# Attention feeding a squared-ReLU MLP: first q loads on a second hardware DMA queue, scalar loads moved to GpSimd's queue, last tile stored as 384 and 128 columns

## Chip, cores, metric

One core of one Trainium2 chip. The metric is the device time of one execution in microseconds (us), median over several executions.

## The reference, cut to what matters

```python
# q, k, v: (4, 8, 768, 64) float32; n_global 8, n_local 96
scores = q @ k.T / 8 + bias(head slope, distance)     # ALiBi-like
scores = where(local or global, scores, -1e9)
attn   = softmax(scores) @ v                          # -> x: (3072, 512)
h      = maximum(x @ w_in, 0)                         # w_in (512, 2048)
out    = (s * h*h + b) @ w_out                        # w_out (2048, 512); s, b: one number each
```

## The kernel before

The work is cut into 12 tiles of 256 tokens. Tile 0 is loaded as float32 on SyncE's queue (hardware_dynamic in the trace) and cast on chip. Everything else (v, later q and k, both weights) goes through GpSimd's queue (software_dynamic), where each issue keeps GpSimd busy for 0.6 to 1.0 us in the trace, and is cast from float32 to bfloat16 on the way. The head of the program, in the order of issue:

```python
nc.scalar.preload_act_table_set("natural_log_exp_and_others")
...
for nm, half in (("k", 0), ("q", 0), ("k", 1), ("q", 1)):
    nc.sync.dma_start(raw32[...], first(nm, half))       # 256 KB each, float32
... # masks on GpSimd, then its loads:
load_v(0); load_quads(1, "k"); load_quads(1, "q")
load_w_in(0, 8); load_w_in(1, 8); load_v(1)
for i in range(2, 8): load_w_in(i, 8)                    # 8 pieces of 256 columns
load_quads(2, "k"); load_quads(2, "q"); load_v(2)
for i in range(3): load_w_out(i)
def load_scalars():                                      # one number to 128 partitions
    nc.sync.dma_start(s_bc[:], moe_s.to_broadcast((P, 1)))
    nc.sync.dma_start(b_bc[:], moe_b.to_broadcast((P, 1)))
for h in range(H):
    nc.scalar.activation(diag[:, h, :], ident[:], ACT.Copy, scale=...)
... # cut
idle(9, "av")                     # 9 filler matmuls
cast("k", 0, "act"); T_mm(0, 0, "k"); T_ev(0, 0, "k")    # transpose on TensorE
cast("q", 0, "act"); ...
more_loads()                      # k(3), w_out(3), q(3), v(3), tile 4, GpSimd's queue
load_scalars()
```

`load_scalars` stands late in the program text, but SyncE has nothing to do before it except the four loads, so it issues the scalars right behind them.

In the steady part, `period(j)` computes the scores of tile j, first and second linear layer of earlier tiles, and loads tile j+2. `pace(j)` makes GpSimd wait for an early result of the period. `KO` collects the keys of the previous block on VectorE:

```python
def period(j, items, at, late=None):
    SS(j, (0, 1))                            # scores, exp, times template
    if j + 2 < NJ:
        pace(j)                              # GpSimd copies one element of pts[j, 0]
        load_granule(j + 2)                  # k, k, q, q, v, v on GpSimd's queue
    ...
    A(j, 1); SS(j, (2, 3))
    if j + 1 < NJ: KO(j + 1)                 # ko <- kT, 128x1024 bfloat16, SBUF to SBUF
    ...
def P2_end(j, tb):                           # the very last 128 tokens, in two column parts
    for pool, tag, lo, hi in ((ps_a, "scA", 0, 320), (ps_b, "scB", 320, DM)):
        P2_cols(j, tb, ps[:, 0, :], lo, hi)  # 16 matmuls, one VectorE op, one store
```

The softmax here doesn't subtract the row's maximum and nothing guards it: scores larger than these inputs give would overflow.

Of the kernel before, what the change touches and what calls it, by code (L numbers as in the profile page):

```python
# [10 lines left out]
ACT = mybir.ActivationFunctionType  # L11
# [7 lines left out]
def kernel(  # L19
# [13 lines left out]
    nc = tc.nc  # L33
    P = nc.NUM_PARTITIONS

    B, H, S, D = q.shape
    NG = int(n_global)
    NL = int(n_local)
    DM = H * D
# [14 lines left out]
    QSCALE = 1.0 / float(D) ** 0.5  # L54
# [8 lines left out]
    ps_a = ctx.enter_context(tc.tile_pool(name="ps_a", bufs=1, space=bass.MemoryType.PSUM))  # L63
    ps_b = ctx.enter_context(tc.tile_pool(name="ps_b", bufs=1, space=bass.MemoryType.PSUM))
# [17 lines left out]
    def bg(j):  # L82
        return divmod(j, NGR)
# [13 lines left out]
    def load_rows(j, nm):  # L97
        b, g = bg(j)
        src = q if nm == "q" else k
        t = ldp.tile([P, GB, H, D], BF16, name=f"{nm}nat", tag=f"{nm}nat")  # L100
        nat[nm, j] = t
        for i in range(GB):
            sb = g * GB + i
            nc.gpsimd.dma_start(  # L104
                t[:, i, :, :], src[b, :, sb * P : (sb + 1) * P, :].rearrange("h p d -> p h d")
            )

    def load_v(j):
        b, g = bg(j)
        for i in range(GB):  # L110
            sb = g * GB + i
            nc.gpsimd.dma_start(  # L112
                vaug[b][:, sb, :, 0:D],
                v[b, :, sb * P : (sb + 1) * P, :].rearrange("h p d -> p h d"),
            )

    def load_granule(j):
        load_rows(j, "k")
        load_rows(j, "q")
        load_v(j)  # L120
# [13 lines left out]
    def load_w_out(i, n=4):  # L134
        w = FC // n
        nc.gpsimd.dma_start(
            w_out_bf[:, i * w : (i + 1) * w, :], w_out_view[:, i * w : (i + 1) * w, :]
        )


    nc.scalar.preload_act_table_set("natural_log_exp_and_others")
    raw32 = gpool.tile([P, 2, H, GB * D], F32, name="raw32", tag="gT")
    for nm in "kq":
        nat[nm, 0] = ldp.tile([P, H, GB * D], BF16, name=f"{nm}nat", tag=f"{nm}nat")
# [1 line left out]
    def first(nm, half):  # L146
        src = (q if nm == "q" else k)[0, 4 * half : 4 * half + 4, 0:GT, :]
        return src.rearrange("h (p i) d -> p h (i d)", i=GB)

    for nm, half in (("k", 0), ("q", 0), ("k", 1), ("q", 1)):  # L150
        nc.sync.dma_start(raw32[:, "kq".index(nm), 4 * half : 4 * half + 4, :], first(nm, half))

    def cast(nm, half, eng=None):
        hs = slice(4 * half, 4 * half + 4)
# [6 lines left out]
    ident = const.tile([P, P], BF16, name="ident")  # L161
# [42 lines left out]
    def more_loads():  # L204
        load_rows(3, "k")
        load_w_out(3)
        load_rows(3, "q")
        load_v(3)
        load_granule(4)

    s_bc = const.tile([P, 1], F32, name="s_bc")
    b_bc = const.tile([P, 1], F32, name="b_bc")

    def load_scalars():
        nc.sync.dma_start(s_bc[:], moe_s.to_broadcast((P, 1)))
        nc.sync.dma_start(b_bc[:], moe_b.to_broadcast((P, 1)))


    diag = const.tile([P, H, P], BF16, name="diag")
    for h in range(H):  # L220
        nc.scalar.activation(
            diag[:, h, :], ident[:], ACT.Copy, scale=float(2.0 ** (-8.0 * (h + 1) / H) / QSCALE)
        )

    for b in range(B):
        nc.vector.memset(vaug[b][:, :, :, D : D + 1], 1.0)
# [62 lines left out]
    def T_ev(j, half, nm, eng=None, es=(0, 1)):  # L289
        b, g = bg(j)  # L290
        a = 0 if nm == "k" else 1
        if j not in qT:
            qT[j] = qtp.tile([P, HP, GT], BF16, name="qT", tag="qT")
        e0, e1 = es[0], es[-1] + 1
        n = GB if j == 0 else 4
        src = tps[j, half, nm][:, a, e0:e1, :].rearrange("p e (i t) -> p e t i", i=n)
        hs = slice(2 * half + e0, 2 * half + e1)
        dst = kT[b][:, hs, g * GT : (g + 1) * GT] if nm == "k" else qT[j][:, hs, :]
        dst = dst.rearrange("p e (t i) -> p e t i", i=n)
        if eng is None:  # L300
            nc.vector.tensor_copy(dst, src)
        else:
            nc.scalar.copy(dst, src)
# [64 lines left out]
    def SB_mm(j, hp, which=None):  # L368
        ps = sc_tile(j, hp, which)
        n = ncols(j)  # L370
        c0 = 0 if n == 3 * P else P
        m = base[:].rearrange("p a c -> p (a c)")[:, c0 : c0 + n]
        for hi in range(2):
            nc.tensor.matmul(
                ps[:, hi, 0:n], lhsT=diag[:, 2 * hp + hi, :], rhs=m, start=True, stop=False
            )
# [221 lines left out]
    def P2_cols(j, tb, ps, lo, hi):  # L598
        b, g = bg(j)
        flush()  # L600
        for fc in range(FC):
            nc.tensor.matmul(  # L602
                ps[:, 0 : hi - lo],
                lhsT=gT[j][:, fc, tb * P : (tb + 1) * P],
                rhs=w_out_bf[:, fc, lo:hi],
                start=(fc == 0),
                stop=(fc == FC - 1),
            )
        o_sb = work.tile([P, hi - lo], F32, name="o_sb", tag="o_sb", bufs=5)
        nc.vector.scalar_tensor_tensor(  # L610
            out=o_sb[:],
            in0=ps[:, 0 : hi - lo],
            scalar=s_bc[:],
            in1=bvec[:, lo:hi],
            op0=ALU.mult,
            op1=ALU.add,
        )
        t0 = b * S + g * GT + tb * P
        nc.sync.dma_start(out[t0 : t0 + P, lo:hi], o_sb[:])

    def P2_end(j, tb):
        for pool, tag, lo, hi in ((ps_a, "scA", 0, 320), (ps_b, "scB", 320, DM)):
            ps = pool.tile([P, 2, DM], F32, name="ps_2e", tag=tag)
            P2_cols(j, tb, ps[:, 0, :], lo, hi)

# [24 lines left out]
    T_mm(0, 1, "q", "av", True)  # L650
    T_ev(0, 1, "q", None, (0,))
    T_ev(0, 1, "q", None, (1,))
    more_loads()
    load_scalars()
    SB_mm(0, 3)
    S_mm(0, 2, True)
    S_post(0, 2, True)
# [167 lines left out]
    for j in range(4, NJ):  # L825
# [11 lines left out]
        [(P2, l, 4, 0), (P2, l, 5), (P1, m, 0), (P2, l, 6), (P1, m, 1), (P2, l, 7), (P1, m, 2), (P1, m, 3), (P1, m, 4)]  # L837
        + [(P2, m, 0), (P1, m, 5), (P1, m, 6), (P1, m, 7), (P2, m, 1), (P2, m, 2), (P2, m, 3)]
        + [(P2_end, m, 1)],
        100,  # L840
    )
# [35 lines left out]
```

## Time and profile before

| | before |
|---|---|
| median of 3 runs | 217.13 us (216.68 to 217.26) |
| span in the profile | 215.4 us |
| TensorE busy | 206.1 us, 96% |
| k0, q0, k1, q1 landed (first and second halves of tile 0) | 3.77, 4.65, 6.80, 7.82 us |
| first v piece, first and sixth w_in piece landed | 9.07, 14.19, 23.64 us |

Landing is the issue time plus "issue to landing" of the trace. All times count from the start of the span. In the views PE is TensorE, PEld its weight loads, DVE VectorE, ACT ScalarE, POOL GpSimd, SP SyncE; a q behind an engine is its sequencer, which issues and waits. L12 is line 12 of the kernel.

The page of the kernel before: the span, busy time by engine, the chain's shares by engine, and two DMA issue groups (size of one, median us from issue to landing).

```profile
span 215.4 us, 5089 instructions
PE 206.1 (96%) x2061; PEld 140.6 (65%) x2093; DVE 135.8 (63%) x322; ACT 115.5 (54%) x176; POOL 69.8 (32%) x96
PE 80%; DMA 9%; ACT 3%; POOL 3%; issue 2%; DVE 1%; SPq 1%; POOLq 0%; ACTq 0%
...
raw<-in_k_dram SPq DMA_DIRECT2D x2, 256.0 KB, 4.0
raw<-in_q_dram SPq DMA_DIRECT2D x2, 256.0 KB, 4.4
```

TensorE bounds the kernel. Only the head, where it waits for data, and the tail after its last matmul can shrink by such a change.

The timeline of SyncE's queue in the first 10 us of the kernel before: start us, us, what.

```profile
0.74 0.46 SPq L151 DMA_DIRECT2D raw<-in_k_dram  x1
1.26 0.49 SPq L151 DMA_DIRECT2D raw<-in_q_dram  x1
1.80 0.50 SPq L151 DMA_DIRECT2D raw<-in_k_dram  x1
2.35 0.51 SPq L151 DMA_DIRECT2D raw<-in_q_dram  x1
2.89 0.57 SPq L215 DMA_DIRECT2D s_bc<-in_moe_s_dram  x1
3.50 0.59 SPq L216 DMA_DIRECT2D b_bc<-in_moe_b_dram  x1
```

One issue takes about 0.5 us of the sequencer; the scalars follow the four loads at once.

The chain of waits of the kernel before in its first 40 us: start us, us, what.

```profile
2.49 6.58 DMA vaug<-in_v_dram
9.07 0.28 issue
...
11.36 2.20 POOL w_in_bf L130 x3
13.56 10.08 DMA w_in_bf<-in_moe_w_in_dram
...
23.68 2.81 PE ps L508 x24
```

The chain runs over GpSimd's stream until 23.64 us, not over q and k. The waits of the weight loads (PEld) between 12 and 30 us in the kernel before, total us, times, longest:

```profile
PEld L508 <- DMA w_in_bf<-in_moe_w_in_dram: 0.7, 3, 0.3
```

The DMA queues of the kernel before from 7 to 8 us: packets, MB, share of 16 engines' time. q0 is GpSimd's queue, q1 SyncE's.

```profile
q0 software_dynamic: 425, 0.05, 83.3%
q1 hardware_dynamic: 194, 0.01, 22.6%
```

In this microsecond the scalars' four-byte packets run on q1 beside GpSimd's stream, which moves 425 packets.

The end of VectorE's timeline of the kernel before: the last two instructions, each followed by a store.

```profile
210.77 0.55 DVE L610 SCALAR_TENSOR_TENSOR o_sb<-ps_2e,s_bc,bvec 128x320 f32<-128x320 f32 x1 [1.42 <-PE ps_2e L602]
212.09 0.42 DVE L610 SCALAR_TENSOR_TENSOR o_sb<-ps_2e,s_bc,bvec 128x192 f32<-128x192 f32 x1 [0.77 <-PE ps_2e L602]
```

### The profile page before, as it was taken

The numbers are of one execution on the slowest core, as the hardware profiler recorded it, in microseconds if no ns is written. First come the engines' busy times: TensorE is split into PE (matmuls) and PEld (weight loads), VectorE is DVE, ScalarE is ACT, GpSimd is POOL, SyncE is SP. The second block draws the span as 40 slices with busy tenths as digits, with TensorE's granted clock in tenths as the row PEclk, the third lists the DMA queues.
The fourth block names the chain that finished last, engine by engine and source line by source line (L and its number), as shares of the span: only waits on it lengthen the run. The fifth ranks groups of instructions, "written<-read, shape, count | busy, mean of one in ns | idle before, by whom it ended". The sixth has DMA issues, their size and how long they took to land.

```text
span 215.4 us, 5089 instructions
## 1 busy us (share of the span) xinstructions
PE 206.1 (96%) x2061; PEld 140.6 (65%) x2093; DVE 135.8 (63%) x322; ACT 115.5 (54%) x176; POOL 69.8 (32%) x96
## 2 busy tenths in 40 slices
PE   7889999999999999999999999999999999999993
PEld 2456877447756766766766766766766766765763
DVE  3576557599889676656756766645756766642431
ACT  7559799444837545544545645544545635541420
POOL 8785593540543607208109008106300000000000
PEclk9999999999999999999999999999999999999999
DMA  6999999999999979999979999958995131031102
GB/s 164 137 186 194 194 193 194 179 152 147 105 137 216 137 118 113 193 145 112 203 130 101 113 179 117 178 77 114 157 146 101 51 97 49 3 97 52 49 0 97
DMA packets 105223, 27.60 MB, mean 128 GB/s; under 512 B 91760, under 2 KB 102256, under 8 KB 105200
## 3 DMA queue, kind: packets, MB, share of 16 engines
q0 software_dynamic: 70912, 13.11, 77.0%
q1 hardware_dynamic: 34288, 14.17, 33.3%
q8 instruction: 16, 0.26, 0.5%
q14 instruction: 7, 0.06, 0.1%
HBM read 27.26 MB, written 6.29 MB: 156 GB/s over the span
## 4 chain that ended last, share of the span: by engine, by line
PE 80%; DMA 9%; ACT 3%; POOL 3%; issue 2%; DVE 1%; SPq 1%; POOLq 0%; ACTq 0%
PE ps L508 35%; PE ps L551 30%; DMA w_in_bf<-in_moe_w_in_dram 5%; PE ps_s L390 5%; PE ps_av L435 4%; PE ps_2s L551 3%; DMA vaug<-in_v_dram 3%; DMA xT<-xn 2%; PE ps_2e L602 2%; POOL w_in_bf L130 1%; ACT gT L517 1%; ACT tmpl L250 1%; POOL vaug L112 1%; SPq L488 1%; ACT pt L403 1%
## 5 line engine op out<-in xcount | busy, mean ns | idle before, releaser
L508 PE MATMUL ps<-xT,w_in_bf 128*128 128x256 bf16 x768 | 94.8, 273 | 0.6 <-DMA xT<-xn 0.2
L517 ACT ACTIVATE gT<-ps 128x512 bf16<-128x512 f32 x96 | 57.3, 599 | 59.8 <-PE ps L508 59.2
L508 PEld LDWEIGHTS <-w_in_bf 128*128 128x128 bf16 x768 | 73.1, 98 | 19.0 <-issue 0.8
L551 PE MATMUL ps<-w_out_bf,gT 128*128 128x512 bf16 x308 | 78.4, 379 | 1.9 <-issue 0.8
L499 DVE TENSOR_TENSOR gT<-gT 128x512 bf16<-128x512 bf16 x96 | 40.0, 421 | 24.1 <-ACT gT L517 23.9
L403 ACT ACTIVATE pt<-ps_s 128x1024 bf16<-128x1024 f32 (+1 forms) x48 | 43.1, 952 | 19.5 <-PE ps_s L390 19.4
L551 PEld LDWEIGHTS <-gT 128*128 128x128 bf16 x368 | 33.6, 98 | 30.3
L407 DVE TENSOR_TENSOR pt<-pt,tmpl 128x1024 bf16<-128x1024 bf16 (+1 forms) x40 | 26.1, 652 | 12.8 <-ACT pt L403 11.7
L112 POOL DMA_DIRECT2D vaug<-in_v_dram x24 | 21.5, 912 | 6.6 <-DMA w_out_bf<-in_moe_w_out_dram 2.7
L562 DVE SCALAR_TENSOR_TENSOR o_sb<-ps,s_bc,bvec 128x512 f32<-128x512 f32 x18 | 13.5, 748 | 12.6 <-PE ps L551 12.6
L444 DVE TENSOR_TENSOR xn<-ps_av,rc 128x256 bf16<-128x256 f32 x48 | 20.4, 424 | 1.7
L435 PEld LDWEIGHTS <-pt 128*128 128x128 bf16 x352 | 16.0, 98 | 6.6 <-DVE xn L444 2.2
L435 PE MATMUL ps_av<-vaug,pt 128*128 128x65 bf16 x224 | 17.4, 193 | 0.9 <-DVE rc L443 0.6
L443 DVE RECIPROCAL rc<-ps_av 128x4 f32<-128x4 f32 x48 | 8.7, 181 | 15.1 <-PE ps_av L435 14.8
L126 POOL COPY pdum<-xT 1x1 bf16<-1x1 bf16 x5 | 0.9, 177 | 50.4 <-DMA xT<-xn 50.4
L104 POOL DMA_DIRECT2D knat<-in_k_dram x18 | 15.8, 883 | 4.3 <-issue 2.3
L104 POOL DMA_DIRECT2D qnat<-in_q_dram x18 | 15.9, 900 | 1.4 <-DMA w_out_bf<-in_moe_w_out_dram 1.4
L390 PE MATMUL ps_s<-qT,kT 64*128 64x128 bf16 x224 | 12.4, 218 | 0.2
L435 PE MATMUL ps_av<-vo,pt 128*128 128x65 bf16 x128 | 12.0, 194 | 0.0
L390 PEld LDWEIGHTS <-kT 64*128 64x128 bf16 x224 | 7.1, 94 | 6.2 <-issue 5.2
L390 PE MATMUL ps_s<-qT,ko 64*128 64x128 bf16 x128 | 8.0, 216 | 0.0
L551 PE MATMUL ps_2s<-w_out_bf,gT 128*128 128x512 bf16 x30 | 7.6, 379 | 0.1
(72 smaller groups left out, 105.3 us busy)
## 6 DMA issues: line engine op xcount, KB each, us to landing
out_dram<-o_sb SPq DMA_DIRECT2D x23, 256.0 KB, 3.4
vaug<-in_v_dram POOLq DMA_DIRECT2D x24, 128.0 KB, 7.3
knat<-in_k_dram POOLq DMA_DIRECT2D x22, 128.0 KB, 5.1
qnat<-in_q_dram POOLq DMA_DIRECT2D x22, 128.0 KB, 6.6
w_in_bf<-in_moe_w_in_dram POOLq DMA_DIRECT2D x8, 256.0 KB, 9.1
w_out_bf<-in_moe_w_out_dram POOLq DMA_DIRECT2D x4, 512.0 KB, 10.0
raw<-in_k_dram SPq DMA_DIRECT2D x2, 256.0 KB, 4.0
raw<-in_q_dram SPq DMA_DIRECT2D x2, 256.0 KB, 4.4
```

Of the source, the lines that this page charges most:

```text
L104: nc.gpsimd.dma_start(t[:, i, :, :], src[b, :, sb * P : (sb + 1) * P, :].rearrange("h p d -> p h d"))
L112: nc.gpsimd.dma_start(vaug[b][:, sb, :, 0:D], v[b, :, sb * P : (sb + 1) * P, :].rearrange("h p d -> p h d"),)
L390: nc.tensor.matmul(ps[:, hi, oc * P : (oc + 1) * P], lhsT=kt[r, :], rhs=qT[j][r, hp, i * P : (i + 1) * P], start=not biased, stop=not bias ...
L403: nc.scalar.activation(pt[:, :, 0:n], ps[:, :, 0:n], ACT.Exp, scale=QSCALE)
L407: nc.vector.tensor_tensor(pt[:, :, 0:n], pt[:, :, 0:n], m, ALU.mult)
L435: nc.tensor.matmul(av[:, i, hi, :], lhsT=pt[:, hi, c * P : (c + 1) * P], rhs=vv, start=n_ == 0, stop=n_ == len(ops) - 1,)
L444: nc.vector.tensor_tensor(xn[j][:, :, 2 * hp : 2 * hp + 2, :], av[:, :, :, 0:D], rc[:].to_broadcast((P, GB, 2, D)), ALU.mult,)
L499: nc.vector.tensor_tensor(gs, gs, gs, ALU.mult)
L508: nc.tensor.matmul(ps[:, i, :], lhsT=w_in_bf[:, kc, fc * P : (fc + 1) * P], rhs=xT[j][:, kc, :], start=(kc == 0), stop=(kc == KC - 1),)
L517: nc.scalar.activation(gs, ps[:], ACT.Relu)
L551: nc.tensor.matmul(po[j, tb], lhsT=gT[j][:, fc, tb * P : (tb + 1) * P], rhs=w_out_bf[:, fc, :], start=(fc == 0), stop=(fc == FC - 1),)
L562: nc.vector.scalar_tensor_tensor(out=o_sb[:], in0=po[j, tb], scalar=s_bc[:], in1=bvec[:], op0=ALU.mult, op1=ALU.add,)
```

## The change

Intent: get q and k issued in half the time by using two queues; keep the scalars out of the way at the start; make the last piece of work after the last matmul smaller. ScalarE now spends time issuing, so its table load comes later, and half of its diag scalings go to VectorE.

```diff
-    nc.scalar.preload_act_table_set("natural_log_exp_and_others")
...
-    for nm, half in (("k", 0), ("q", 0), ("k", 1), ("q", 1)):
-        nc.sync.dma_start(raw32[:, "kq".index(nm), ...], first(nm, half))
+    for half in range(2):
+        for a, (nm, eng) in enumerate((("k", nc.sync), ("q", nc.scalar))):
+            eng.dma_start(raw32[:, a, ...], first(nm, half))
+    nc.scalar.preload_act_table_set("natural_log_exp_and_others")
...
-        nc.sync.dma_start(s_bc[:], moe_s.to_broadcast((P, 1)))
-        nc.sync.dma_start(b_bc[:], moe_b.to_broadcast((P, 1)))
+        nc.gpsimd.dma_start(s_bc[:], moe_s.to_broadcast((P, 1)))
+        nc.gpsimd.dma_start(b_bc[:], moe_b.to_broadcast((P, 1)))
...
     for h in range(H):
-        nc.scalar.activation(diag[:, h, :], ident[:], ACT.Copy, scale=...)
+        make_diag(h, "act" if h >= 4 else "dve")
...
-        for pool, tag, lo, hi in ((ps_a, "scA", 0, 320), (ps_b, "scB", 320, DM)):
+        for pool, tag, lo, hi in ((ps_a, "scA", 0, 384), (ps_b, "scB", 384, DM)):
...
+    load_scalars()
     more_loads()
-    load_scalars()
```

On GpSimd's queue the scalars now stand between the third w_out piece and k(3).

More of the change, by code (lines that the diff above doesn't have):

```diff
@@ L148, in first @@
         return src.rearrange("h (p i) d -> p h (i d)", i=GB)
-    for nm, half in (("k", 0), ("q", 0), ("k", 1), ("q", 1)):
-        nc.sync.dma_start(raw32[:, "kq".index(nm), 4 * half : 4 * half + 4, :], first(nm, half))
+    for half in range(2):
+        for a, (nm, eng) in enumerate((("k", nc.sync), ("q", nc.scalar))):
+            eng.dma_start(raw32[:, a, 4 * half : 4 * half + 4, :], first(nm, half))
+    nc.scalar.preload_act_table_set("natural_log_exp_and_others")
     def cast(nm, half, eng=None):
@@ L214, in load_scalars, with make_diag @@
     def load_scalars():
-        nc.sync.dma_start(s_bc[:], moe_s.to_broadcast((P, 1)))
-        nc.sync.dma_start(b_bc[:], moe_b.to_broadcast((P, 1)))
+        nc.gpsimd.dma_start(s_bc[:], moe_s.to_broadcast((P, 1)))
+        nc.gpsimd.dma_start(b_bc[:], moe_b.to_broadcast((P, 1)))
     diag = const.tile([P, H, P], BF16, name="diag")
+    def make_diag(h, eng):
+        scale = float(2.0 ** (-8.0 * (h + 1) / H) / QSCALE)
+        if eng == "act":
+            nc.scalar.activation(diag[:, h, :], ident[:], ACT.Copy, scale=scale)
+        else:
+            nc.vector.tensor_scalar_mul(diag[:, h, :], ident[:], scale)
     for h in range(H):
-        nc.scalar.activation(
-            diag[:, h, :], ident[:], ACT.Copy, scale=float(2.0 ** (-8.0 * (h + 1) / H) / QSCALE)
-        )
+        make_diag(h, "act" if h >= 4 else "dve")
     for b in range(B):
```

## The prediction

> **What bounds the kernel now.** TensorE. The page gives PE 206.1 us busy of a 215.4 us span (96%) at full clock, and the chain of waits puts 80% of the span on PE. From about 50 us on, the timeline has PE back to back. So the change can only win in the first 24 us and in the last 7.
>
> The head has three limits. (a) The first float32 halves: from the timeline, SyncE issues k0, q0, k1, q1 at 0.74, 1.26, 1.80, 2.35 us (about 0.5 us each), and their consumers stop waiting at 3.80 (k0), 4.67 (q0), 6.83 (k1) and 7.84 us (q1). The late pair sets the second half of the first scores (9.44 us). (b) v(0), on GpSimd's queue, lands from 9.07 us. (c) The weight stream: the chain runs over w_in from 13.56 to 23.64 us, and PE's weight loads wait for w_in at 14.23 (0.29 us), 20.98 (0.17) and 23.68 (0.27). A gain in (a) that doesn't also move (c) is lost at 23.7 us.
>
> **What the change does.**
> 1. q0 and q1 go out on ScalarE's queue at about 0.74 and 1.26 us, so all four issues are out by about 1.8 instead of 2.85 us. DMA by slices shows the engines near idle at 2.2-2.4 us and then 320-350 GB/s, so I expect the 1 MB to be moved about 0.5 us earlier. The Trainium skill, "DMA: Bandwidth & Descriptors", section "Issuing engines are not separate DMA queues", says queues share the 16 engines and only issue time is saved; so k0 now shares with q0. Estimates: k0 ready about 4.3 us (0.5 later), q0 4.3 (0.35 earlier), k1 about the same, q1 about 6.9 (0.9 earlier). First scores 0.3 us later, second 0.5 earlier.
> 2. The table load (1.28 us in the trace) starts about 1 us later, at 1.8 us, ends about 3.1; four diag scalings remain on ScalarE (0.21 each), done about 3.95, before k0. Neutral.
> 3. The two scalar loads leave SyncE's queue. Packet counts: some 250 four-byte packets run from 6.5 to 8.5 us beside GpSimd's loads, whose packet rate doubles when they end. Removing them should move v and w_in earlier by 0.2-0.6 us. Added back at about 28 us: two GpSimd issues (I estimate 0.6-0.9 us each, as its other loads) ahead of k(3). q(3)'s transposes land about 52.6 us and PE reads them at 53.8, so about 1 us of slack; the earlier stream should offset it.
> 4. Tail: last column part 192 -> 128. VectorE took 418 ns for 192 and 551 for 320, so 128 takes about 350: 0.07 us saved; last store (1.7 us to landing for 96 KB) at most 0.1 us shorter. PE work equal (3.5 us). Gain 0.1 us.
>
> **Sum.** Head 0.4-0.5 us kept at 24 us, tail 0.1: 217.1 -> 216.5 us, within 2%. Range 215.8 to 217.2.
>
> **What would show it.** ScalarE's k cast later (about 4.3), VectorE's q1 cast earlier (about 6.9); the first P1 matmul about 13.9 instead of 14.2-14.6; the w_in wait near 23.7 ending 0.3-0.6 us earlier; last VectorE op near 350 ns.
>
> **What would make it wrong.** The w_in stream does not move, and the gain disappears at 23.7 us; VectorE's diags delay GpSimd's masks and thus v's issue; k0's delay dominates; the added GpSimd issues push q(3) past 53.8 us and PE stalls; or two queues overlap better than I think, giving over 1 us.

## The result

| | before | changed |
|---|---|---|
| median us (6 runs each) | 216.91 (216.40 to 217.60) | 216.72 (216.45 to 216.85) |
| ratio, 95% interval | | 0.9989 [0.9969, 1.0009] |

A ratio is the mean time of one kernel's fast runs over that of the other's fast runs of the same rounds, so it is not quite the ratio of the medians. The measured time lies in the predicted range, but the gain is 0.2 us instead of 0.6, and the interval includes none.

The page of the changed kernel, the same lines, and its new queue q10 (ScalarE's):

```profile
span 215.0 us, 5118 instructions
PE 208.3 (97%) x2093; PEld 140.3 (65%) x2093; DVE 136.1 (63%) x326; ACT 114.7 (53%) x172; POOL 70.8 (33%) x98
q10 hardware_dynamic: 1056, 0.52, 0.9%
PE 85%; ACT 5%; DVE 4%; DMA 3%; issue 1%; SPq 1%; DVEq 0%; ACTq 0%
...
raw<-in_q_dram ACTq DMA_DIRECT2D x2, 256.0 KB, 4.8
raw<-in_k_dram SPq DMA_DIRECT2D x2, 256.0 KB, 4.2
```

DMA fell from 9% of the chain to 3%. (The PE counts differ because 32 matmul records are missing in the first trace, not because work was added: the weight loads number 2093 in both.) From issue to landing k0 takes 3.60 us instead of 3.03 and q0 4.06 instead of 3.39; k1 (4.78, 5.00) and q1 (5.45, 5.47) are hardly quicker. The late pair lands sooner because it is issued sooner.

The timeline of ScalarE in the head of the changed kernel:

```profile
0.74 1.11 ACTq L151 DMA_DIRECT2D raw<-in_q_dram  x2
1.88 1.28 ACT L152 ACT_TABLE_LOAD   x1 [1.88 <-issue]
3.17 0.91 ACT L224 ACTIVATE diag<-ident 128x128 bf16<-128x128 bf16 x4
4.37 0.62 ACT L160 CAST knat<-raw 128x512 bf16<-128x512 f32 x1 [0.29 <-DMA raw<-in_k_dram]
4.89 0.61 ACT L160 CAST qnat<-raw 128x512 bf16<-128x512 f32 x1
```

The later table load and the diag scalings end before k0 arrives, so they cost nothing. k0's cast starts at 4.37 instead of 3.80 us: it now shares the engines with q0.

The chain of waits of the changed kernel in the head:

```profile
0.74 3.60 DMA raw<-in_k_dram
...
9.40 0.67 PE ps_s L396 x12
...
14.39 1.05 PE ps L514 x8
...
23.01 2.64 PE ps L514 x24
```

The chain no longer touches w_in. It now runs from k0 through the first scores and the engines. TensorE's group at 23.68 us before is at 22.85 us here (its weight loads start at 22.79). The wait list of the weight loads has no line for w_in any more.

The DMA queues of the changed kernel from 7 to 8 us; q1 has no packets:

```profile
q0 software_dynamic: 816, 0.18, 195.2%
```

GpSimd's stream moves 816 packets instead of 425 and 0.18 MB instead of 0.05. The first w_in piece lands at 12.03 us (14.19), the sixth at 21.27 (23.64).

The end of VectorE's timeline of the changed kernel:

```profile
210.81 0.62 DVE L616 SCALAR_TENSOR_TENSOR o_sb<-ps_2e,s_bc,bvec 128x384 f32<-128x384 f32 x1 [1.85 <-PE ps_2e L608]
211.70 0.35 DVE L616 SCALAR_TENSOR_TENSOR o_sb<-ps_2e,s_bc,bvec 128x128 f32<-128x128 f32 x1 [0.28 <-PE ps_2e L608]
```

**Following the lag.** Set one instruction's start in the changed kernel against the same instruction's in the kernel before. VectorE's sixth squaring (of h, after the first linear layer; "the squaring" below), near 25 us, is 0.85 us ahead (24.55 against 25.40). The bvec instruction (VectorE scales the bias row, once), near 64 us, is only 0.50 ahead (63.78 against 64.28), and the last VectorE instruction 0.39 ahead; these last 0.11 us go near 146 us, where TensorE waits for a DMA of x. So two questions are open. Which part of the change moved the weight stream by 2.2 us, when 0.2 to 0.6 was predicted? And who took 0.35 us back near 62 us?

The place of the second loss. Before, VectorE's and GpSimd's timelines there:

```profile
60.60 0.42 DVE L334 COPY ko<-kT 128x1024 bf16<-128x1024 bf16 x1
...
56.35 1.75 POOL L104 DMA_DIRECT2D knat<-in_k_dram  x2 [0.35 <-issue]
...
59.81 1.79 POOL L112 DMA_DIRECT2D vaug<-in_v_dram  x2
```

The changed kernel, the same lines:

```profile
59.76 0.76 DVE L340 COPY ko<-kT 128x1024 bf16<-128x1024 bf16 x1
...
55.90 1.75 POOL L104 DMA_DIRECT2D knat<-in_k_dram  x2 [0.72 <-issue]
...
59.36 1.79 POOL L112 DMA_DIRECT2D vaug<-in_v_dram  x2
```

The ko copy takes 0.76 us instead of 0.42. It starts 0.40 us into GpSimd's v issue (59.76 - 59.36) instead of 0.79, because GpSimd's first k issue started 0.72 us after the pacing copy instead of 0.35. The weight loads then wait for VectorE, from 60 to 64 us, before:

```profile
PEld L435 <- DVE xn L444: 0.5, 1, 0.5
```

and in the changed kernel:

```profile
PEld L441 <- DVE xn L450: 0.9, 1, 0.9
```

That is the 0.35 us, to within rounding.

### The profile page after: what moved, and what is told of

Read it like the earlier page. It is cut to its first block, busy times and chain, and to the rows that moved or that the text cites. A ratio compares the mean times of both kernels' runs of the same rounds, so it can differ in the third digit from the quotient of the medians.

```text
span 215.0 us, 5118 instructions
## 1 busy us (share of the span) xinstructions
PE 208.3 (97%) x2093; PEld 140.3 (65%) x2093; DVE 136.1 (63%) x326; ACT 114.7 (53%) x172; POOL 70.8 (33%) x98
## 4 chain that ended last, share of the span: by engine, by line
PE 85%; ACT 5%; DVE 4%; DMA 3%; issue 1%; SPq 1%; DVEq 0%; ACTq 0%
PE ps L514 36%; PE ps L557 31%; PE ps_s L396 5%; PE ps_av L441 5%; PE ps_2s L557 3%; ACT pt L409 2%; DMA xT<-xn 2%; DMA raw<-in_k_dram 2%; PE ps_2e L608 2%; DVE xn L450 1%; PE ps_s L380 1%; ACT gT L523 1%; ACT tmpl L256 1%; SPq L494 1%; PE ps_t L272 1%
## 5 line engine op out<-in xcount | busy, mean ns | idle before, releaser
L557 PE MATMUL ps<-w_out_bf,gT 128*128 128x512 bf16 x336 | 82.6, 379 | 0.0
```

Of the source, the lines that this page charges most:

```text
L557: nc.tensor.matmul(po[j, tb], lhsT=gT[j][:, fc, tb * P : (tb + 1) * P], rhs=w_out_bf[:, fc, :], start=(fc == 0), stop=(fc == FC - 1),)
```

## The experiments

All gave correct results and ran at five rounds unless noted. The first four shared one chip, the next four another, the last four a third.

### e1_scal: only the scalars moved

```diff
 # kernel before
-        nc.sync.dma_start(s_bc[:], ...); nc.sync.dma_start(b_bc[:], ...)
+        nc.gpsimd.dma_start(s_bc[:], ...); nc.gpsimd.dma_start(b_bc[:], ...)
-    more_loads()
     load_scalars()
+    more_loads()
```

> The kernel before with one part of the change: the two scalar loads moved to GpSimd's queue behind w_out. Theory S (the scalar packets on SyncE's queue hold back GpSimd's stream): the first w_in piece lands near 12.2 us (14.2 before, 12.0 with the whole change), the sixth near 21.5 (23.6 before, 21.3 after), no wait for w_in is left on PE, and q's second half lands near 7 instead of 7.8 us. VectorE's squaring at 25.4 us comes 0.5 to 0.9 us earlier. Rival Q (the earlier end of the q and k loads moves the stream): w_in lands at 13.7 us or later, and under 0.3 us is left at 25 us. Time within 0.3 us of the changed kernel under S, of the kernel before under Q.

Measured: first w_in piece at 12.79 us, sixth at 22.11, no wait for w_in, q1 at 7.42 us, squaring at 24.68 (0.72 earlier). Theory S's numbers, a little weak. But at 62 us the ko copy took 752 ns, the gap on GpSimd was 724 ns, and the lag fell to 0.39 us. Time 216.53 us, ratio 0.9983 [0.9956, 1.0011].

### e2_qact: only q on ScalarE's queue (with table load and diags)

```diff
 # kernel before, plus the q/k, table and diag lines of the change
 # scalars stay early on SyncE's queue, tail stays 320 and 192
```

> The kernel before with the other part: q halves on ScalarE's queue, the table load after them, four diag scalings on VectorE; scalars stay early on SyncE's queue, the tail as before. Theory S: first scores 0.3 to 0.4 us later (k's first half shares with q's), but w_in still lands at 13.5 us or later, PE still waits for w_in near 23.5 us, and at 25 us no more than 0.3 us is gained. Rival Q: w_in lands near 12.3 us and 0.6 to 0.9 us is gained at 25 us.

Measured: first scores 0.46 us later (ScalarE's first exponential of the scores, "exp" below, at 7.29 against 6.83), but w_in at 12.35 and 21.53 us, squaring at 24.64 (0.76 earlier). Those are rival Q's numbers. So each half of the change alone moves the stream by 1.4 to 1.8 us, and together 2.2: they largely remove the same thing. S and Q both fall as written. The DMA queues of e2_qact from 7 to 8 us show why; q1 has no packets here either:

```profile
q0 software_dynamic: 964, 0.17, 224.3%
```

With q1 half as long, SyncE's scalar packets are through by about 6 us (255 four-byte packets fall between 5.5 and 6.0 us in the packet records), when GpSimd's stream has hardly begun. In the kernel before they come between 6.5 and 8.5 us, in the middle of it. Hence a new theory, I: what costs is scalars *taking turns* with the stream. (GpSimd is not the cause: it issues the first w_in piece at 6.80 to 6.84 us in before, changed, e1_scal and e2_qact.)

e2_qact kept its gain at 62 us (ko copy 421 ns, gap 351 ns): 216.31 us, ratio to before 0.9973 [0.9949, 0.9996]. Its median lies 0.4 us below the changed kernel's, but that one was timed in another batch; e12_best makes the comparison on one chip.

### e3_tail: only the tail

```diff
 # kernel before
-        ... (0, 320) ... (320, DM)
+        ... (0, 384) ... (384, DM)
```

> The kernel before with the tail alone in parts of 384 and 128 columns. Last VectorE instruction 351 ns instead of 418, the last store lands 1.58 instead of 1.66 us after its issue, so the end of the chain is 0.1 to 0.15 us earlier after the same start of the last tile. In the time this is below what five rounds can tell (ratio 0.9995, interval across 1).

Measured: last VectorE instruction 351 ns (418), last store 1.60 us to landing (1.66). From its start to the landing that is 1.98 us against 2.10: 0.12 us, as expected, and invisible in the time (0.9997 [0.9961, 1.0033]). Its head, which is the head of before, had the sixth w_in piece at 22.49 us instead of 23.64 and the squaring at 24.84: a first sign that one profile of a head is one sample. Measured against this one, the changed kernel's stream is 2.1 us earlier at the first piece (12.03, 14.10), but only 1.2 at the sixth.

### e4_vko: GpSimd's v load for tile 5 held until after the ko copy

```diff
 # changed kernel, in period(), for j == 3
-            load_granule(j + 2)
+            load_rows(j + 2, "k"); load_rows(j + 2, "q")   # v later
...
             KO(j + 1)
+            nc.gpsimd.tensor_copy(pdum[:], kos[j + 1][0:1, 0, 0, 0:1])
+            load_v(j + 2)
```

> The changed kernel, with GpSimd's v load for tile 5 issued after VectorE's ko copy for tile 4 instead of beside it. Theory C (the 0.35 us lost near 62 us is a collision of the ko copy with GpSimd's building of a DMA: copy 759 ns against 422 before, and a start 0.34 us late): the copy takes about 420 ns at about 59.4 us, the lag of the weight loads behind the kernel before stays near -0.85 us at 62 to 66 us, and 0.3 to 0.4 us is gained in the time. Rival D (VectorE is simply behind at that place whatever GpSimd does, or the loss is a DMA wait): the copy is not quicker or the lag still falls to -0.5 us at 62 us. In both, about 0.1 us is lost at 146 us to the transposes of x.

VectorE's and GpSimd's timelines of e4_vko:

```profile
59.86 0.42 DVE L340 COPY ko<-kT 128x1024 bf16<-128x1024 bf16 x1
...
55.99 1.75 POOL L104 DMA_DIRECT2D knat<-in_k_dram  x2 [0.72 <-issue]
...
60.63 0.24 POOL L792 COPY pdum<-ko 1x1 bf16<-1x1 bf16 x1 [1.14 <-DVE ko L343]
```

The gap of 0.72 us is still there, but with no v issue beside it the copy takes 419 ns, the wait of the weight loads is back at 0.5 us, and TensorE's lead over the kernel before, 0.75 us at 25 us, is 0.74 at 66. Theory C holds. The span was 214.4 us against 215.0 of the changed kernel, but only 0.35 us of that is the copy: the changed kernel's profile lost another 0.35 near 146 us, that of e4_vko nothing, and e4_vko's head was 0.1 later. The time was 216.45 us, ratio 0.9981 [0.9956, 1.0005]. The 0.1 us that was also expected to be lost at 146 us did not appear (0.98 ahead there); that wait for a DMA of x varies from profile to profile: 0.24 us in before, none in e10_before.

### e5_scal3: four more scalar loads behind the two (one look)

```diff
 # kernel before, behind the two scalar loads
+        for i in range(4):
+            nc.sync.dma_start(extra_i[:], (moe_s or moe_b).to_broadcast((P, 1)))   # never read
```

> The kernel before with four more scalar loads behind the two on SyncE's queue (three pairs in all, the extra tiles unread). Theory I (a four-byte read that takes turns with GpSimd's small packets on a DMA engine holds that engine): GpSimd's rate stays low as long as the extra scalars run, to 10 us or later, and the first w_in piece lands at 16 us or later (14.2 before). Rival J (the scalars cost only their own packet time of 22 ns, and the slow start is the late end of q's data): 512 more packets over 16 engines are 0.7 us, w_in lands at 14.2 to 14.9 us.

Measured: first w_in piece at 16.47 us. Theory I's number; J falls. One run, 218.97 us.

### e6_qact_scal4: six more scalar loads in e2_qact (one look)

```diff
 # e2_qact, behind the two scalar loads
+        for i in range(6): ...    # as in e5_scal3
```

> The kernel of e2_qact (q on ScalarE's queue) with six more scalar loads on SyncE's queue, so that scalars still run when GpSimd's stream has started, which the two of e2_qact do not. Theory I: GpSimd's packets fall from about 600 to 150 to 250 in half a microsecond between 6 and 8.5 us, and the first w_in piece lands at 13.8 us or later, although the q and k data end as early as in e2_qact. Rival J: w_in lands at 12.4 to 13.1 us as in e2_qact (12.35).

The DMA queues of e6_qact_scal4 from 7 to 8 us:

```profile
q0 software_dynamic: 738, 0.10, 147.0%
q1 hardware_dynamic: 127, 0.00, 13.3%
```

q and k ended earlier than in e2_qact (the last at 6.05 us, 6.83 there), yet the first w_in piece landed at 17.76 us instead of 12.35. Theory I again, J falls. The dip in the packet rate was shallower than I wrote (738 packets in this microsecond, not 300 to 500) but lasted longer, past 10 us. So the cost per scalar load beside the stream is (14.19 - 12.79) / 2 = 0.70 us from before and e1_scal, (16.47 - 14.19) / 4 = 0.57 from e5_scal3, (17.76 - 12.35) / 6 = 0.90 from here. The records give such a packet 7 to 22 ns, so 128 of them over 16 engines account for at most 0.18 us. What an engine does in the rest no record here shows. So it is shown that scalar loads beside the stream cost this much; that they do so by taking turns on an engine is not.

The run took 219.82 us. The stretch from 14 to 18 us of its table by windows (start and end, length, busy time of PE, PEld, DVE, ACT, POOL, granted clock, DMA share, GB/s):

```profile
14.00:18.00 4.00, 4.00 (x82) 2.40 (x83) 2.40 (x7) 1.66 (x3) 2.39 (x4) 0.57 1.84 181
```

TensorE was busy for 0.31 of the 2 us from 12 to 14, and then its clock was halved from 14.35 to 17.76 us. That bears on the spread, below.

### e7_best: the whole change but the scalars' move

```diff
 # e2_qact
-        ... (0, 320) ... (320, DM)
+        ... (0, 384) ... (384, DM)
```

> Everything of the change but the move of the scalars: q on ScalarE's queue, diags split, scalars early on SyncE's queue, tail 384 and 128. If e2_qact's profile repeats (no loss at 62 us because GpSimd's queue is not shifted) and e3_tail's 0.1 us adds, the time is 216.2 us, 0.3 to 0.5 us below the changed kernel, with the ko copy at 420 ns. If e2_qact was luck, it is the changed kernel's 216.7 us.

Measured: 216.21 us, ratio 0.9977 [0.9962, 0.9991], ko copy 419 ns, gap 349 ns. As expected for a real gain, of 0.2%.

### e8_pool4: two more scalar loads on GpSimd's queue

```diff
 # changed kernel, behind the two scalar loads
+        for i in range(2): nc.gpsimd.dma_start(extra_i[:], ...)   # never read
```

> The changed kernel with two more scalar loads on GpSimd's queue beside the two that it moved there (unread). The changed kernel's third k load after the pacing copy waits 724 ns at 55 us, 350 without scalars on that queue, with all its semaphores done. Theory P (the extra 375 ns belong to the place in the rotation of eight DMA semaphores, which two loads more shift to the one where the trace of the changed kernel has the wait at 335 ns): the gap is 330 to 360 ns, the ko copy takes about 420 ns and nothing is lost at 62 us, so it is about 0.35 us faster than the changed kernel in spite of more work. Rival R (any shift of GpSimd's queue costs it, or the queue is simply later): the gap stays at 700 ns or the ko copy at 750 ns, and the loss stays.

Measured: gap 701 ns, ko copy 748 ns, weight loads waiting 0.9 us for VectorE, 216.89 us, ratio 1.0017 [0.9991, 1.0043]. Theory P falls; rival R describes it. Why GpSimd's first k issue comes 0.35 us later stays open: its semaphores had long been reached.

### e10_before, e11_after, e12_best, e9_warm10: repeats, and one more filler matmul

```diff
 # e10_before, e11_after, e12_best: kernel before, changed kernel, e7_best, unchanged
 # e9_warm10: e7_best with
-    idle(9, "av")
+    idle(10, "av")
```

> The kernel before once more, unchanged, for a second profile of its head and for the spread of its time against itself. If the profile of before was a late sample (e3_tail, whose head is the same, had its sixth w_in piece 1.15 us earlier and stood 0.6 us ahead at 24 us), the squaring at 25.4 us comes 0.3 to 0.8 us earlier here, with the first w_in piece at 14.0 to 14.4 us all the same. Ratio 1.000.

> The changed kernel once more, for a second profile. The first w_in piece lands at 11.9 to 12.6 us, the GpSimd gap after the pacing copy is 724 ns, the ko copy takes 750 ns and 0.3 to 0.4 us is lost at 62 us again. Ratio to before 0.998 to 0.9995.

> e7_best once more beside the changed kernel on one chip. If its gain is real: 0.3 to 0.5 us below e11_after, ratio to before about 0.9975, gap 350 ns and ko copy 420 ns in the profile.

> e7_best with ten instead of nine filler matmuls ahead of the first transposes, since k's first half now lands later and TensorE sits idle before it (0.26 us in the changed kernel, 0.55 in e7_best) while its clock comes up anywhere between 3.6 and 6.8 us in the profiles. If the idle time holds the clock back, the clock comes up before 5 us and the time falls by 0.1 to 0.2 us against e12_best with less spread; if the moment is free of what TensorE does, there is no difference, or 0.1 us more from the later first transposes.

| | w_in 1st, 6th landed | squaring | ko copy ns | GpSimd gap ns | bvec at | span | median us | ratio, 95% |
|---|---|---|---|---|---|---|---|---|
| before | 14.19, 23.64 | 25.40 | 422 | 349 | 64.28 | 215.4 | 216.91 | |
| e10_before | 14.09, 23.53 | 25.29 | 420 | 350 | 64.16 | 215.1 | 216.80 | 1.0018 [0.9971, 1.0064] |
| changed | 12.03, 21.27 | 24.55 | 759 | 724 | 63.78 | 215.0 | 216.72 | 0.9989 [0.9969, 1.0009] |
| e11_after | 12.18, 21.26 | 24.64 | 755 | 724 | 63.90 | 214.8 | 216.79 | 0.9989 [0.9962, 1.0017] |
| e3_tail | 14.10, 22.49 | 24.84 | 419 | 349 | 63.71 | 214.7 | 216.50 | 0.9997 [0.9961, 1.0033] |
| e2_qact | 12.35, 21.53 | 24.64 | 421 | 351 | 63.53 | 214.4 | 216.31 | 0.9973 [0.9949, 0.9996] |
| e7_best | 12.55, 21.83 | 24.96 | 419 | 349 | 63.85 | 214.6 | 216.21 | 0.9977 [0.9962, 0.9991] |
| e12_best | 12.47, 21.71 | 24.67 | 422 | 350 | 63.56 | 214.4 | 216.31 | 0.9984 [0.9948, 1.0020] |

My expectation for e10_before was wrong: the first profile of before was not a late sample, the repeat is within 0.11 us of it, and e3_tail was the odd one. e11_after repeats the loss at 62 us in every number. e12_best is 0.48 us below e11_after in the median on one chip. Its interval is wide because one of its runs took 218.24 us and two runs of before took 217.77 and 218.27. e9_warm10: 216.47 us, ratio 0.9977 [0.9949, 1.0004], not better than e12_best (in its profile an earlier ko copy, at 31.80 us, took 778 ns and cost 0.12 us). The clock came up at 3.63 us there and at 4.04 in e12_best, which one look each cannot tell from chance.

**Spread.** Of 45 runs with the head of before whose clock is listed (33 of before in the three batches, e10_before, e3_tail), six had a mean granted clock of 0.992 or less, and took 217.77 to 219.14 us. Of 54 runs with the scalars or q moved (changed kernel, e1, e2, e4, e7 to e9, e11, e12), none was below 0.997. A deficit of 0.008 over 215 us is 3.4 us at half clock, the length of the dip in e6_qact_scal4. That a TensorE waiting for w_in also causes dips in the slow runs of before is possible but not shown: none of those runs was the profiled one, and e5_scal3, whose TensorE was busy for 0.47 of the 2 us from 10 to 12, shows no dip. Two of the 54 runs were over 218 us at full clock, for a reason not found.

## Why the prediction was right or wrong

The total was right (216.72 in 215.8 to 217.2, "within 2%"), but partly by luck, because errors cancelled; and the range also holds the kernel before (216.91), so that hitting it says little.

- *"k0 ready about 4.3 us (0.5 later)"*: 4.34. *"q1 about 6.9"*: 6.69. *"q0 4.3"*: wrong, 4.80, a bit later than before (4.65). *"k1 about the same"*: wrong, 6.04 instead of 6.80. *"First scores 0.3 us later"*: 0.36. *"second 0.5 earlier"*: the exp of the second pair came only 0.19 earlier (9.79 against 9.98), and against e10_before (9.69) it came later.
- *The table load and diags neutral*: right, ScalarE waited 0.29 us for k0 after them.
- *"Removing them should move v and w_in earlier by 0.2-0.6 us"*: **this term was mis-sized.** Alone it moves w_in by 1.4 us (e1_scal). I had the observation in hand (the stream's packet rate doubles when the scalars end) and still priced it near the scalars' own packet time. Repeating the loads shows 0.6 to 0.9 us per load.
- I also treated terms 1 and 3 as separate. e2_qact shows that moving q does nearly the same to the stream, because it lets the scalars finish before the stream begins.
- *"Head 0.4-0.5 us kept at 24 us"*: more came, 0.65 to 0.85 us (changed and e11_after against before and e10_before), but a third or more was **not kept**. Most of the stream's 2.2 us buys nothing: w_in stops being waited for, and the chain falls back on q, k and the first attention. In the profiles of changed, e1, e2, e4, e11, e12 and e9 the squaring stands at 24.55 to 24.68 us, whether the sixth w_in piece landed at 21.3 or 22.1 (in e7 and e8, whose first exps were late, at 24.96 and 25.23).
  The kept traces show which limit took over. ScalarE's exps of the first and second pair, before:

```profile
6.83 1.51 ACT L403 ACTIVATE pt<-ps_s 128x768 bf16<-128x768 f32 x2 [0.44 <-PE ps_s L390]
9.98 1.51 ACT L403 ACTIVATE pt<-ps_s 128x768 bf16<-128x768 f32 x2 [1.64 <-PE ps_s L390]
```

  and changed:

```profile
7.19 1.51 ACT L409 ACTIVATE pt<-ps_s 128x768 bf16<-128x768 f32 x2 [0.44 <-PE ps_s L396]
9.79 1.51 ACT L409 ACTIVATE pt<-ps_s 128x768 bf16<-128x768 f32 x2 [1.08 <-PE ps_s L396]
```

  In ten of the 14 profiles (all but before, e10, e5 and e6) the squaring comes 14.76 to 14.77 us after the second pair's exp, wherever w_in stands. In before, e10, e5 and e6 it comes later, 1.76 us after the sixth w_in piece lands (1.84 in e6). And the second pair's exp comes 2.59 or 2.60 us after the first in all 11 profiles whose q1 landed by 7.42 us. So of the 0.85 us about 0.66 is w_in no longer waited for and 0.19 the exp. Bringing q1 below 7.4 us bought nothing more, and the later k0 was passed on in full: beside what it did for the stream, moving q gained 0.19 us against before and nothing against e10_before, whose q1 landed at 7.41. An estimate, not run: with e1_scal's stream and the first exp at 6.83, as in before, the squaring would stand at 24.2 us (6.83 + 2.59 + 14.77).
- *"the added GpSimd issues push q(3) past 53.8 us and PE stalls"* was the listed danger of moving the scalars to GpSimd. q(3) was in time. The cost came at a place that I had not looked at: GpSimd's queue 0.35 us later in its phase, the ko copy caught behind its v issue, TensorE 0.35 us later. e4_vko shows the collision by removing it, e1_scal and e8_pool4 show that it comes with the scalars on that queue.
- *"Gain 0.1 us" in the tail, 350 ns*: 351 ns, 0.12 us from the last instruction's start to the landing (e3_tail).

So the sum was: head +0.7, collision -0.35, tail +0.1, a few tenths in all, of which 0.2 shows in the medians. Left out of the account is TensorE's start. The Trainium skill, "TensorE: Matmul & The Clock Gate", section "Part 1: The HAM clock gate (the "warmup" mystery)", says that the window that raises the clock runs free, so the moment varies from run to run. In the 14 profiles the clock came up between 3.63 us (e3_tail, e9_warm10) and 6.76 us (e8_pool4). In e8_pool4 the first transposes took 314 ns each instead of 219, and its squaring stood at 25.23 us although w_in was as early as in the changed kernel. Differences of 0.3 us between two single profiles of a head can be this alone. The 0.35 us at 62 us can't: they are read between two points of the same profile.

For the collision the skill has the mechanism. "SBUF — State Buffer", section "Who interferes with whom", says that VectorE's copies in their two-port modes share a port pair with GpSimd, that the pair is an exclusive lock, and that the later one blocks fully. The traces agree with the blocking, both ways, for the ko copies of this size in the 14 profiles. The eight that start 0.31 to 0.42 us into a load that GpSimd is issuing take 680 to 778 ns, one that starts at 0.60 us takes 476. Those that start later, from 0.69 us on, take 416 to 422 ns. Five near 32 us start early, 0.06 to 0.19 us into one: they take 420 to 423 ns, but GpSimd's issue takes 957 to 1095 ns, where the others that overlap this copy take 878 to 911. In before nothing is lost because the copy starts at 0.79 us of the v issue. That this copy runs in a two-port mode no record says. "DMA: Bandwidth & Descriptors", section "Issuing engines are not separate DMA queues", from which I had argued, says that the DMAs of all issuing engines run on the same 16 DMA engines; the trace agrees (k0, now beside q0, takes 3.60 us to land instead of 3.03), but it led me to leave out what stands behind whom in a queue, and when.

The version that comes out ahead of both kernels is e7_best: 216.21 and 216.31 us in two batches, against 216.78 and 216.82 for before on the same chips, and 216.79 for the changed kernel on the second of them. Only the first batch's interval excludes no gain. Not run was the obvious next one: q left on SyncE's queue and the scalars issued there later, once w_in has landed, which would keep k0 early and leave GpSimd's queue alone.

## What to carry to other kernels

A load of one number to all partitions cost little when it ran ahead of the stream (first w_in piece at 12.35 us in e2_qact, 12.03 in the changed kernel) and 0.6 to 0.9 us per load beside it. Let it finish before the stream begins or issue it where nobody is waiting, and look for such loads right behind the big ones of an idle queue. A queue whose engine also shares a port with VectorE is not a free place to park small work: 0.35 us of shift decided here whether a copy took 420 or 755 ns on TensorE's path. When a stream gets 2 us earlier, ask what the next limit is before crediting the gain; here it stood 0.7 us behind the old one, and it was the load that the change itself had made later, k0.

## What the Trainium skill lacked or had wrong

- "DMA: Bandwidth & Descriptors", section "Issuing engines are not separate DMA queues": it says that issuing from several engines saves only issue time. It lacks what that time can be worth to a later load: with q on ScalarE's queue SyncE issued the scalars at 1.81 instead of 2.89 us, behind two loads instead of four, and the first w_in piece on a third queue landed at 12.35 instead of 14.19 us.
- The same page gives no price for a broadcast of one number to 128 partitions beside a GpSimd stream: 0.57, 0.70 and 0.90 us per load of 0.5 KB in three comparisons.
- "TensorE: Matmul & The Clock Gate", section "Part 1: The HAM clock gate (the "warmup" mystery)": it puts the transition around 4 us, ±500 ns run to run. In 14 profiles with the first matmul at 0.78 us the clock came up from 3.63 to 6.76 us after the start of the span, so 2.85 to 5.98 us after that matmul. The length of its window (3413 ns) agrees with the dip in e6_qact_scal4 (14.35 to 17.76 us).
- "SBUF — State Buffer", section "Who interferes with whom": it says that the first to issue holds the pair for its whole instruction. Here a 128x1024 bfloat16 copy of 420 ns took 748 to 759 ns when it started 0.40 to 0.42 us into GpSimd's v issue of about 0.91 us, but was not slowed when it started 0.78 us into one: by the records' starts and ends, which are rough for GpSimd, the pair was free before the issue ended.
- "ScalarE: Activation LUTs", section "What ACT_TABLE_LOAD costs": 1283 ns agrees (1.28 us), but the drain of about 1380 ns that it adds did not show behind the changed kernel's load: the next activation started 0.01 us after its end (1.88 + 1.28, then 3.17). This load is the kernel's only one and ScalarE's first work; what one in the midst of work costs no run here shows.
- No page has it: with the scalar loads on GpSimd's queue, its first DMA behind the pacing copy of period 3 came 701 to 724 ns after it (five profiles) instead of 348 to 351 (nine profiles), with all semaphores reached. The cause is open.
